# A piece of weights is begun six rooms or more behind its fetch, and its absolute value keeps its traced place in ScalarE's order

## The chip, the core and the metric

One core of a Trainium2 chip runs the whole program. The metric is the device time of one execution in microseconds; the time before is the median of three runs. TensorE (PE) multiplies, VectorE (DVE) and ScalarE (ACT) work elementwise, GpSimd (POOL) does some elementwise work and issues accumulating DMAs, SyncE (SP) issues most other DMAs.

## The reference

```python
def _attn_ref(q, k, v, lam):            # q, k, v: (2, 8, 768, 64), lam: (8,)
    for b in range(nb):                 # blocks of 64 tokens
        intra = einsum('bhic,bhjc->bhij', qb, kb) * Dmask      # Dmask: lam ** (i - j), i >= j
        intra = einsum('bhij,bhjd->bhid', intra, vb)
        inter = einsum('bhid,bhde->bhie', qb * lam_pow, kv_state)
        out[:, :, sl] = intra + inter
        kv_state = lam_block * kv_state + einsum('bhsd,bhse->bhde', kb * rev_pow, vb)
...
x = attn_out.transpose(0, 2, 1, 3).reshape(1536, 512)
h = maximum(x @ w_in, 0.0);  x = h * h @ w_out          # first MLP, 512 -> 2048 -> 512
h = x @ w_in2;  out = maximum(0.01 * h, h) @ w_out2     # second MLP
```

The four weight matrices of the two MLPs (512 x 2048 and 2048 x 512) come as float64, that is as two 32-bit words for each weight.

## The kernel before

**Stages.** First the attention part: twelve units of 128 tokens, in `retention`. Then two MLPs of four stages each, a stage being 512 of the 2048 hidden columns; tokens go in three tiles of 512. Stage (l, s) is stage s of layer l. Every product of the MLPs is three matmuls (`three`, L503): each operand is split into a high and a low part, and high*high, high*low and low*high are summed. In the second and third stage of layer 0, and in all of layer 1, pairs of tiles are multiplied with seven products in place of eight (`second_pair`, `first_pair`), which needs sums of weights (`weight_sums`, L437 to L442) and of activations (`four_sums`, L449 to L451).

**Weights.** Each of the 8 stages has four pieces of weights, 32 in all: two halves of its first matrix and two of its second. `order` lists them; they are numbered 1 to 32 here. A piece is fetched by `fetch` (1 MB, by SP's queue, into one of two buffers `raw`) and made from float64 words into a high and a low part by the generator `converting`: an absolute value on ACT (L114), six steps on DVE (L115, L116, L118, L121, L122, L125), a copy on ACT that makes the high part (L135), and a subtraction on DVE that makes the low part (L137); some pieces then, or before the copy, have their sums made. Behind L122 the raw buffer is free, and `converting` issues the next fetch, that of the piece two further on. Before the copy it waits, giving None, until `opened` holds the piece, that is until the matmuls that read the old contents of the buffer have been traced.

**Rooms.** The matmuls of the MLPs are written by generators (`first`, `first_pair`, `second_pair`, `second`) that yield after every six matmuls, half a group of twelve; each yield but those that give False is a room, in which `convert` is called once. A call gives one step of the first piece at work that has one; if none has, it begins the next fetched piece, which traces the absolute value and the first DVE step together. In the attention part there are seven rooms, at the ends of units 3 to 9 (`convert(pin=True)`), for piece 1. Rooms are numbered 1 to 355 here in the order of the calls; room 8 is the first of the MLPs.

**Order.** The program is traced in this order, and the order of each engine is then made by a planner that takes instructions when it thinks them ready, by priority, with its own idea of durations. PE's order in the MLPs is as traced (`manual_schedule`); ACT's and DVE's are the planner's. `keep_in_program_order(i)` puts instruction i behind the one that was traced just before it on the same engine. `high_priority` pulls some of the sums and splits forward. A queue runs in the order that it was given, and an instruction whose inputs aren't there holds all behind it.

Of the kernel before, what the change touches and what calls it, by code (L numbers as in the profile page):

```python
# [9 lines left out]
F32 = mybir.dt.float32  # L10
# [3 lines left out]
AF = mybir.ActivationFunctionType  # L14
# [5 lines left out]
def tile_retention_then_two_mlps(  # L20
# [12 lines left out]
    nc = tc.nc  # L33
# [30 lines left out]
    def dma(dst, src):  # L64
        return nc.sync.dma_start(dst, src)
# [7 lines left out]
    def source(l, s, n, h):  # L73
        w = ((w1, w2), (w3, w4))[l][n]
        if n == 0:
            return w[:, s * FS + h * CW:s * FS + (h + 1) * CW].rearrange("(k p) f -> p k f", p=P)
        return w[s * FS + h * CW:s * FS + (h + 1) * CW, :].rearrange("(k p) f -> p k f", p=P)
# [6 lines left out]
        order += [(*stage, 1, 0), (*stage, 0, 0), (*stage, 0, 1)]  # L84
    order.append((*stages[-1], 1, 1))
    todo = list(order)
    fetched, at_work = [], []
    wts, sums, opened = {}, {}, set()

    def fetch():  # L90
        if todo:
            key = todo.pop(0)
            r = raw.tile([P, 4 * CW], I64, tag="raw", name="raw")
            k = 4 if key[2] == 0 else 2
            dma(r.rearrange("p (k f) -> p k f", k=k), source(*key))
            fetched.append((key, r))

    def converting():
        key, r = fetched.pop(0)
        l, s, n, h = key  # L100
        k = 4 if n == 0 else 2
        words = r.bitcast(U32).rearrange("p (f t) -> p f t", t=2)
        w_lo, w_hi = words[:, :, 0], words[:, :, 1]
        ve = nc.vector
        if not apart(key):
            hb = cv.tile([P, 4 * CW], U32, tag="hb", name="hb", bufs=2)
        else:
            if h == 0:
                opened_memory[s] = late.tile([P, 2, 4 * CW], U32, tag="sw1", name="hb")
            hb = opened_memory[s][:, h]  # L110
        rb = cv.tile([P, 4 * CW], U32, tag="rb", name="rb")
        hf, rf = hb.bitcast(F32), rb.bitcast(F32)

        nc.scalar.activation(hf, w_hi.bitcast(F32), AF.Abs)  # L114
        yield ve.tensor_scalar(out=hf, in0=hf, scalar1=2.0 ** -15, scalar2=122368.0, op0=ALU.max, op1=ALU.min)  # L115
        yield ve.tensor_scalar(out=hb, in0=hb, scalar1=3, scalar2=0x3FFFFFFF,  # L116
                               op0=ALU.logical_shift_left, op1=ALU.bitwise_and)
        yield ve.scalar_tensor_tensor(out=hb, in0=w_hi, scalar=0xC0000000, in1=hb,  # L118
                                      op0=ALU.bitwise_and, op1=ALU.bitwise_or)

        yield ve.tensor_scalar(out=rb, in0=hb, scalar1=0xFF800000, scalar2=None, op0=ALU.bitwise_and)  # L121
        yield ve.scalar_tensor_tensor(out=rf, in0=w_lo, scalar=2.0 ** -52, in1=rf, op0=ALU.mult, op1=ALU.mult)  # L122
        if begun_mlp:
            fetch()
        yield ve.tensor_tensor(out=hf, in0=hf, in1=rf, op=ALU.add)  # L125
        if l == 1 and n == 0:
            w = hf.rearrange("p (k f) -> p k f", k=k)
            blocks = {(i, j): w[:, 2 * j:2 * j + 2, i * P:(i + 1) * P] for i in range(2) for j in range(2)}
            yield from weight_sums(key, f"sw{h}", blocks, rf)
        while key not in opened:  # L130
            yield None
        tags = (f"w1h{h}", f"w1l{h}") if n == 0 else ("w2h", "w2l")
        bufs = 1 if n == 0 else 3
        hi, lo = (wp.tile([P, 4 * CW], F32R, tag=tag, name=tag, bufs=bufs) for tag in tags)
        nc.scalar.copy(hi, hf)  # L135
        wts[key] = [x.rearrange("p (k f) -> p k f", k=k) for x in (hi, lo)]
        yield ve.tensor_tensor(out=lo, in0=hf, in1=hi, op=ALU.subtract)  # L137
        if (l, s) in seven and n == 1:
            while ("sums", l, s) not in opened:
                yield None  # L140
            rb = cv.tile([P, 4 * CW], U32, tag="rb", name="rb")
            w = hf.rearrange("p (k m i f) -> p k m i f", k=2, m=2, i=2)
            blocks = {(i, j): w[:, j, :, i] for i in range(2) for j in range(2)}
            yield from weight_sums(key, f"t{h + 2}", blocks, rb.bitcast(F32))
# [4 lines left out]
    def apart(key):  # L149
        return key[0] == 0 and key[1] > 1 and key[2] == 1  # L150


    def convert(pin=False):
        for piece in list(at_work):
            step = next(piece[1], False)
            if step is False:
                at_work.remove(piece)
            elif step is not None:
                if pin:
                    tc.keep_in_program_order(step)  # L160
                return
        if not fetched:
            return
        key = fetched[0][0]
        alike = sum(apart(k) == apart(key) for k, _ in at_work)
        if alike < (2 if not apart(key) or key[3] == 1 else 1):
            at_work.append((key, converting()))
            step = next(at_work[-1][1])
            if pin:
                tc.keep_in_program_order(step)  # L170
# [3 lines left out]
    begun_mlp = []  # L174
# [9 lines left out]
    def retention(ctx_att, att):  # L184
# [206 lines left out]
        for i in range(n_units):  # L391
            if i and i + 2 < n_units:
                scale_q(i + 2, transposes(i + 2))
            if i + 4 < n_units:
                load(i + 4, "kq")
            if i + 2 < n_units:
                load(i + 2, "v")
            if i in (1, 9):
                fetch()
            if i:  # L400
                if i > 1:
                    state(i)
                output(i)
                if i + 1 < n_units:
                    mask(i + 1)
                if i + 2 < n_units:
                    scores(i + 2)
            if 3 <= i <= 9:
                convert(pin=True)
# [22 lines left out]
    def weight_sums(key, tag, a, f):  # L432
        both = late.tile([P, 2, 4, 2, P], F32R, tag=tag, name="sw")
        sums[key] = both
        f = f.rearrange("p (n k f) -> p n k f", n=4, k=2)
        ve = nc.vector
        ve.tensor_tensor(out=f[:, 0], in0=a[1, 0], in1=a[1, 1], op=ALU.add)  # L437
        yield ve.tensor_tensor(out=f[:, 2], in0=a[0, 0], in1=a[1, 0], op=ALU.subtract)
        ve.tensor_tensor(out=f[:, 1], in0=f[:, 0], in1=a[0, 0], op=ALU.subtract)
        yield ve.tensor_tensor(out=f[:, 3], in0=a[0, 1], in1=f[:, 1], op=ALU.subtract)  # L440
        nc.scalar.copy(both[:, 0], f)
        yield ve.tensor_tensor(out=both[:, 1], in0=f, in1=both[:, 0], op=ALU.subtract)  # L442
# [305 lines left out]

    begun_mlp.append(True)
    fetch()  # L750
    opened.update(order[:7])
    opened.add(("sums", 0, 1))
    with tc.manual_schedule(engines={mybir.EngineType.PE}):
        for l, s in stages:
            for part in stage(l, s):
                for room in part:
                    if room is not False:
                        convert()
# [25 lines left out]
```

## Time and profile before

| | us |
|---|---|
| median of 3 runs (lowest, highest) | 576.34 (575.51, 576.9) |
| the profiled execution's own time | 577.1 |
| its span, first to last instruction | 575.3 |
| PE busy | 566.2 (98%) |
| DVE busy | 413.8 (72%) |
| ACT busy | 303.7 (53%) |
| POOL busy | 103.3 (18%) |
| mean granted TensorE clock | 0.994 |

The span is 1.8 us shorter than the execution's time. Busy times are sums over the whole span; the stages differ in which engine has room left. The profile tells for each idle time what ended it, and the timeline view has every instruction with its start.

### The profile page before, as it was taken

Reading aid. Unit: us, or ns where it says so; the run is one execution under the profiler, and the core shown is the slowest. Engines: PE = TensorE matmul, PEld = TensorE weight load, DVE = VectorE, ACT = ScalarE, POOL = GpSimd, SP = SyncE. Lnnn points to the kernel's source line nnn. Section 1 sums busy time; section 2 is a strip of 40 time slices with the busy share of each in tenths; the row PEclk is TensorE's granted clock in tenths of the full one; section 3 lists DMA queues with packets and bytes.
Section 4 is the critical chain, followed back from the end, with each engine's and each line's share of the span. In section 5 each row is a group of like instructions: output and inputs, shape, how many; then the busy total and the mean of one; then the engine's idle time right before and its main releaser. Section 6 shows DMA issues by size and latency. Waiting matters only on the chain.

```text
span 575.3 us, 8060 instructions
## 1 busy us (share of the span) xinstructions
PE 566.2 (98%) x3075; PEld 472.8 (82%) x3075; DVE 413.8 (72%) x579; ACT 303.7 (53%) x477; POOL 103.3 (18%) x115
## 2 busy tenths in 40 slices
PE   7999999999999999999999999999999999999997
PEld 6888888888788888888888888888888888888886
DVE  3588999999927599498478999929782996217222
ACT  2344598556757587757448375453562376225110
POOL 3659100000044503433000000000213010210000
PEclk9899999999999999999999999999999999999999
DMA  8998434665498957999513215341529423651432
GB/s 173 235 218 177 142 130 140 221 190 186 171 157 137 161 168 176 214 254 188 174 38 91 81 34 216 129 164 73 110 49 246 108 32 43 78 87 56 164 111 91
DMA packets 79350, 80.75 MB, mean 140 GB/s; under 512 B 40264, under 2 KB 51792, under 8 KB 79312
## 3 DMA queue, kind: packets, MB, share of 16 engines
q1 hardware_dynamic: 61312, 62.15, 35.2%
q0 software_dynamic: 17472, 17.83, 22.9%
q8 instruction: 24, 0.39, 0.3%
q10 hardware_dynamic: 528, 0.26, 0.2%
q14 instruction: 14, 0.11, 0.1%
HBM read 55.05 MB, written 30.42 MB: 149 GB/s over the span
## 4 chain that ended last, share of the span: by engine, by line
PE 79%; DVE 10%; DMA 5%; issue 3%; ACT 2%; POOL 1%; SPq 0%; ACTq 0%; POOLq 0%; DVEq 0%
PE ps L503 72%; DMA raw<-in_moe_w_in 4%; PE ps L294 2%; DMA raw<-in_moe_w_out 2%; DVE hb L118 2%; PE ps L311 1%; DVE rb L122 1%; DVE hb L125 1%; PE ps L362 1%; DVE hb L115 1%; DVE rb L121 1%; PE ps L335 1%; ACT hb L114 1%; PE ps L220 1%; PE ps L360 1%
## 5 line engine op out<-in xcount | busy, mean ns | idle before, releaser
L503 PE MATMUL ps<-xhi,w1h 128*128 128x512 f32 x288 | 112.2, 389 | 0.0
L503 PE MATMUL ps<-xhi,w1l 128*128 128x512 f32 x288 | 112.0, 389 | 0.0
L503 PE MATMUL ps<-xlo,w1h 128*128 128x512 f32 x288 | 112.0, 389 | 0.0
L616 POOL DMA_DIRECT2D spill<-f x48 | 47.1, 1194 | 348.3 <-ACT f L612 348.2
L612 ACT COPY f<-ps 128x512 f32<-128x512 f32 x84 | 48.4, 585 | 69.6 <-PE ps L503 68.8
L503 PEld LDWEIGHTS ps<-xhi,w1l 128*128 128x128 f32 x288 | 54.1, 188 | 11.3
L503 PEld LDWEIGHTS ps<-xlo,w1h 128*128 128x128 f32 x288 | 54.1, 188 | 11.3
L503 PEld LDWEIGHTS ps<-xhi,w1h 128*128 128x128 f32 x288 | 54.0, 188 | 11.3 <-issue 0.2
L474 DVE TENSOR_TENSOR g0l<-f,g0h 128x512 fp32r<-128x512 f32 x52 | 35.1, 687 | 32.5 <-ACT f L470 20.9
L503 PE MATMUL ps<-w2l,g0h 128*128 128x512 f32 (+1 forms) x132 | 50.5, 383 | 0.0
L503 PE MATMUL ps<-w2h,g0l 128*128 128x512 f32 (+1 forms) x132 | 50.5, 383 | 0.0
L503 PE MATMUL ps<-w2h,g0h 128*128 128x512 f32 (+1 forms) x132 | 50.5, 383 | 0.0
L114 ACT ACTIVATE hb<-raw 128x1024 f32<-128x1024 f32 x32 | 36.8, 1149 | 21.5 <-DVE w2l L137 8.3
L137 DVE TENSOR_TENSOR w2l<-hb,w2h 128x1024 fp32r<-128x1024 f32 x16 | 19.5, 1222 | 39.8 <-ACT w2h L135 39.8
L503 PE MATMUL ps<-g0h,w2h 128*128 128x512 f32 x104 | 40.5, 389 | 0.0
L503 PE MATMUL ps<-g0l,w2h 128*128 128x512 f32 x104 | 40.5, 389 | 0.0
L503 PE MATMUL ps<-g0h,w2l 128*128 128x512 f32 x104 | 40.5, 389 | 0.0
L122 DVE SCALAR_TENSOR_TENSOR rb<-raw,rb 128x1024 f32<-128x1024 uint32 x32 | 39.4, 1231 | 0.4
L125 DVE TENSOR_TENSOR hb<-hb,rb 128x1024 f32<-128x1024 f32 x32 | 39.4, 1231 | 0.4
L118 DVE SCALAR_TENSOR_TENSOR hb<-raw,hb 128x1024 uint32<-128x1024 uint32 x32 | 39.1, 1221 | 0.3
L567 DVE TENSOR_TENSOR f<-ps,f 128x512 f32<-128x512 f32 x40 | 26.2, 684 | 9.9 <-PE ps L503 9.9
L716 DVE TENSOR_TENSOR f<-ps,f 128x512 f32<-128x512 f32 (+1 forms) x25 | 16.7, 668 | 22.9 <-PE ps L503 22.8
(143 smaller groups left out, 1155.0 us busy)
## 6 DMA issues: line engine op xcount, KB each, us to landing
raw<-in_moe_w_in SPq DMA_DIRECT2D x16, 1024.0 KB, 5.7
raw<-in_moe_w_out SPq DMA_DIRECT2D x16, 1024.0 KB, 5.1
spill<-f POOLq DMA_DIRECT2D x48, 256.0 KB, 5.5
spill<-f SPq DMA_DIRECT2D x24, 256.0 KB, 2.8
f<-spill SPq DMA_DIRECT2D x24, 256.0 KB, 3.0
k<-in_k SPq DMA_DIRECT2D x12, 256.0 KB, 5.0
q<-in_q SPq DMA_DIRECT2D x12, 256.0 KB, 5.1
v<-in_v SPq DMA_DIRECT2D x12, 256.0 KB, 5.3
```

Of the source, the lines that this page charges most:

```text
L114: nc.scalar.activation(hf, w_hi.bitcast(F32), AF.Abs)
L118: yield ve.scalar_tensor_tensor(out=hb, in0=w_hi, scalar=0xC0000000, in1=hb, op0=ALU.bitwise_and, op1=ALU.bitwise_or)
L122: yield ve.scalar_tensor_tensor(out=rf, in0=w_lo, scalar=2.0 ** -52, in1=rf, op0=ALU.mult, op1=ALU.mult)
L125: yield ve.tensor_tensor(out=hf, in0=hf, in1=rf, op=ALU.add)
L137: yield ve.tensor_tensor(out=lo, in0=hf, in1=hi, op=ALU.subtract)
L294: nc.tensor.transpose(ps[:, p, :], src[:, 2 * p:2 * p + 2, :].rearrange("s h d -> s (h d)"), ident)
L474: nc.vector.tensor_tensor(out=glo, in0=r, in1=ghi, op=ALU.subtract)
L503: nc.tensor.matmul(ps, a, b, start=start and n == 0, stop=stop and n == len(ops) - 1, skip_group_check=again)
L567: ve.tensor_tensor(out=out, in0=ps[h, where], in1=other, op=ALU.add)
L612: nc.scalar.copy(f, src)
L616: nc.gpsimd.dma_start(dst, f, accum_op=ALU.add)
L716: nc.vector.tensor_tensor(out=a, in0=ps, in1=a, op=ALU.add)
```

## The change

Two things. A fetch notes the room from which its piece may be begun: six rooms behind the room of the fetch for those issued once the MLPs have begun, at once for the earlier ones; `convert` counts its calls and begins no piece before that. And the absolute value of every piece is put behind the ACT instruction that was traced just before it.

```diff
-    fetched, at_work = [], []
+    fetched, at_work, rooms = [], [], []
+    LAND = 6
...
             dma(r.rearrange("p (k f) -> p k f", k=k), source(*key))
-            fetched.append((key, r))
+            fetched.append((key, r, len(rooms) + LAND if begun_mlp else 0))
 
     def converting():
-        key, r = fetched.pop(0)
+        key, r, _ = fetched.pop(0)
...
-        nc.scalar.activation(hf, w_hi.bitcast(F32), AF.Abs)
+        tc.keep_in_program_order(nc.scalar.activation(hf, w_hi.bitcast(F32), AF.Abs))
...
     def convert(pin=False):
+        rooms.append(len(rooms))
         for piece in list(at_work):
...
-        if not fetched:
+        if not fetched or len(rooms) < fetched[0][2]:
             return
```

## Rows read from the trace of the kernel before

**Rows 1.** The page's first part: busy time, share, instructions.
```profile
PE 566.2 (98%) x3075; PEld 472.8 (82%) x3075; DVE 413.8 (72%) x579; ACT 303.7 (53%) x477; POOL 103.3 (18%) x115
```

**Rows 2.** Waits of PE: waiter, releaser, us in total, times, longest.
```profile
PE ps L503 <- DVE g1l L69: 0.9, 1, 0.9
PE ps L311 <- ACT qT L298: 0.4, 2, 0.2
```

**Rows 3.** Timeline of PE, start of the MLPs and stage (0, 1): start, us.
```profile
65.07 0.40 PE L503 MATMUL ps<-xhi,w1h 128*128 128x512 f32 x1
...
153.49 0.39 PE L503 MATMUL ps<-g1h,sw 128*128 128x512 f32 x1
...
153.95 0.88 PE L503 MATMUL ps<-g1h,sw 128*128 128x512 f32 x2
155.74 0.50 PE L503 MATMUL ps<-g1l,sw 128*128 128x512 f32 x1 [0.92 <-DVE g1l L69]
...
156.54 0.40 PE L503 MATMUL ps<-g1l,sw 128*128 128x512 f32 x1
```

**Rows 4.** Timeline of ACT, piece 9's absolute value and before the stop.
```profile
115.58 1.17 ACT L114 ACTIVATE hb<-raw 128x1024 f32<-128x1024 f32 x1 [1.54 <-DMA raw<-in_moe_w_out]
...
148.37 0.62 ACT L68 CAST t<-f 128x512 fp32r<-128x512 f32 x1 [1.26 <-DVE f L450]
...
150.10 0.58 ACT L482 ACTIVATE f<-ps 128x512 f32<-128x512 f32 x1
150.71 0.63 ACT L486 ACTIVATE f<-f 128x512 f32<-128x512 f32 x1
...
153.65 0.62 ACT L68 CAST g1h<-f 128x512 fp32r<-128x512 f32 x1 [1.82 <-DVE f L491]
```

**Rows 5.** Timeline of DVE before the stop.
```profile
151.80 1.22 DVE L125 TENSOR_TENSOR hb<-hb,rb 128x1024 f32<-128x1024 f32 x1
152.93 0.69 DVE L491 TENSOR_TENSOR f<-f 128x512 f32<-128x512 f32 x1
...
154.66 0.42 DVE L440 TENSOR_TENSOR rb<-hb,rb 128x256 f32<-128x256 f32 x1
155.00 0.69 DVE L69 TENSOR_TENSOR g1l<-f,g1h 128x512 fp32r<-128x512 f32 x1
```

**Rows 6.** Busy time by stretch: stretch, length, PE, PEld, DVE, ACT, POOL, clock.
```profile
60.00:155.74 95.74, 94.82 (x466) 78.41 (x460) 92.55 (x119) 65.55 (x98) 0.40 (x1) 1.00 0.48 161
155.74:180.00 24.26, 24.26 (x107) 20.08 (x108) 10.44 (x15) 16.48 (x29) 11.82 (x12) 1.00 0.92 156
```

**Rows 7.** Line 122 alone, from the start to 155.74 us.
```profile
L122 DVE SCALAR_TENSOR_TENSOR rb<-raw,rb x12: 1214/1218/1560, 47.3 to 150.1; 128x1024 f32<-128x1024 uint32 x12
```

**Rows 8.** Groups of DVE, 60 to 155.74 us: busy us, mean ns, idle before.
```profile
L115 DVE TENSOR_SCALAR hb<-hb 128x1024 f32<-128x1024 f32 x11 | 7.6, 687 | 1.4 <-ACT hb L114 1.4
L137 DVE TENSOR_TENSOR w2l<-hb,w2h 128x1024 fp32r<-128x1024 f32 x5 | 6.0, 1218 | 0.0
```

**Rows 9.** Timeline of ACT at the start of the MLPs, and piece 4's copy.
```profile
61.41 1.17 ACT L114 ACTIVATE hb<-raw 128x1024 f32<-128x1024 f32 x1 [2.47 <-DMA raw<-in_moe_w_in]
...
66.65 0.60 ACT L468 ACTIVATE f<-ps 128x512 f32<-128x512 f32 x1 [1.04 <-PE ps L503]
...
68.00 0.63 ACT L470 ACTIVATE f<-f 128x512 f32<-128x512 f32 x1
...
86.43 1.06 ACT L135 CAST w2h<-hb 128x1024 fp32r<-128x1024 f32 x1 [0.72 <-DVE hb L125]
```

**Rows 10.** Waits of ACT for fetched pieces, whole span.
```profile
ACT hb L114 <- DMA raw<-in_moe_w_in: 6.9, 4, 2.5
...
ACT hb L114 <- DMA raw<-in_moe_w_out: 4.5, 4, 1.5
```

**Rows 11.** Timelines of DVE and PE in stage (0, 2).
```profile
217.48 0.69 DVE L69 TENSOR_TENSOR g1l<-f,g1h 128x512 fp32r<-128x512 f32 x1
...
218.45 0.39 PE L503 MATMUL ps<-g1l,sw 128*128 128x512 f32 x1
```

## The prediction

> **What bounds the kernel.** I read the page's busy times first: PE is busy 98% of the span [rows 1]. The waits of PE come next. In the MLPs there is one, of L503 on a low part made by DVE; in the attention part a wait for ACT's copies shows 0.4 us in two places [rows 2]. PE's timeline gives the pace. Room 8 begins at 65.07 and room 73 at 153.49, 65 rooms in 88.42 us, so a room is 1.360 us and a matmul 0.2267; room r begins at 65.07 + 1.360 (r - 8) [rows 3]. The stop stands two lines on. From 153.95 to 156.54 there are five steps, which should take 1.13 us and take 2.59: 1.46 us are lost [rows 3]. PE's order and number of matmuls are not touched by the change. So what can be won is that 1.46 and the little in the attention part, and what can be lost is any new wait of PE.
>
> What made the stop is read from ACT and DVE together. The matmul waited for the low part by L69, which began at 155.00 behind the small weight sums (L437 to L440) [rows 5]. Its high part was copied on ACT at 153.65, after 1.82 us of waiting for L491 [rows 4]. L491 had its input at 151.34, when L486 ended [rows 4], and began at 152.93, behind the conversion step L125 [rows 5]. L482, the head of this chain, belongs to the group that ends when room 69 begins, 148.03; with ACT free it starts 0.22 us behind a group's end (66.65 against room 9 at 66.43 [rows 9]), so it could have started at 148.25. It started at 150.10, since ACT stood before that at a copy which waited for DVE [rows 4]. All of it is one thing: DVE is busy 92.55 of 95.74 us from 60 us on, then 10.44 of 24.26 [rows 6].
>
> And DVE is busy with work that nobody needs yet. By the code, PE is at room 74 when the stop ends, and calls up to room 74 have asked for L122 of pieces 1 to 10; the trace has 12 of them by then [rows 7]. Counted in the code, DVE has done ahead of its room: all six steps of pieces 11 and 12, L125 of piece 10, and sums that the code asks for in rooms 94 and 95. A piece's six steps are three of 1.22 [rows 7] and three of 0.69 [rows 8], 5.7 us; four sums of 0.42 [rows 5] are 1.7; together 11.4 + 1.2 + 1.7 = 14.3 us. The planner could do this because a piece's absolute value hung on nothing but its fetch: piece 9's, asked for in room 63 (139.87), ran at 115.58, and ACT even waited 1.54 us for its data [rows 4].
>
> **The change, part by part.** *The six rooms.* Counting calls: a fetch goes out in the room of a piece's sixth step and is for the piece two further on. If the present piece has its last step free, the next is begun two rooms on and takes seven, so the fetched one is begun nine rooms behind its fetch; if the present piece must wait, the next is begun one room on, and the fetched one seven rooms behind. I find no piece of the 30 concerned nearer than seven. The rule never says no; it costs and gives 0, on both ends, and moves no DMA in the code.
>
> *The pin.* No instruction is added; all 32 absolute values get a place behind the ACT instruction traced before them, which in the MLPs is an activation, copy or keep of the group that PE has just ended, or the copy of the piece before. So from a few us after its room, not before, can a piece be begun. Its first DVE step and the rest follow, and so does the fetch behind L122, later by as much, in SP's queue among the spills. A fetch still has the rooms above, 9.5 us or more at PE's pace, to land. Spills that stand behind a later fetch in SP's queue have nine buffers f, filled one a group (2.72 us), so some 20 us of cover: 0.
>
> *Term 1, the stop at 154.* With pieces 10 to 12 held to rooms 70, 76 and 82 (149.4, 157.6, 165.7), DVE has only piece 9 to mix into the chain. Without others the chain runs 148.25 + 0.58 (L482) + 0.63 (L486) + 0.69 (L491) + 0.62 (copy) + 0.69 (L69), 151.5 with small gaps [rows 4, 5]; it is needed at 153.49 + 4 x 0.2267 = 154.40. Cover 2.9 us, against one 1.22 step in progress ahead of each of the two DVE steps and one absolute value of 1.17 ahead on ACT, 3.6 at the worst, about half as a rule. Bounds: -1.46 and 0; I take -1.2, near the full gain, for the worst mix seldom falls together.
>
> *Term 2, the attention part.* Piece 1's absolute value stood ahead of copies that PE waited for [rows 2]; pinned, it comes behind them. Bounds -0.4 and 0; I take -0.2, since by the timeline one of the two waits stands there.
>
> *Term 3, deadlines in stage (0, 0).* Piece 2: its absolute value moves behind the last copy of the attention part, which ends about 64.3; 64.3 to 65.5 instead of 61.41 [rows 9]. Six steps 5.7, two activations' subtractions of 0.69 between them, copy 1.05, L137 1.22 [rows 8, 9]: ready at 74.9, needed in room 19, 80.0. Piece 3: pinned to the group that ends at room 15 (74.6), whose three activations end 2.2 us later (66.43 to 68.63 [rows 9]); absolute value to 78.0, ready at about 87.3, needed in room 31, 96.4. Piece 4: pinned to piece 3's copy, which ends at 86.1; absolute value to 87.2, six steps and three subtractions to 95.0, copy to 96.0, low part at 97.2; needed at room 32 and two matmuls, 98.16. Left: 0.9 us, and a set of activations (1.98 from L468's start to L470's end [rows 9]) ahead of a copy would overdraw it. Bounds 0 and +3.1 (two sets); I take 0, as in the rows of before the conversion's copy goes ahead of the next group's activations (86.43, piece 4 [rows 9]).
>
> *Term 4, stage (0, 2).* The same chain exists there: L69 ends at 218.17 and PE wants it at 218.45 [rows 11], 0.28 us. The first three steps of pieces 13 and 14 (2.6 us each), which ran before PE was at their rooms, now fall into it. One more 1.22 step ahead costs 0.94, two 2.2. Bounds 0 and +2.2; I take 0, because there too a 1.22 step already stands in the row of the chain.
>
> *Term 5, ACT's waits for fetches,* 11.4 us in eight [rows 10], mostly vanish; PE didn't wait behind them, so 0. From 155.74 on DVE has 13.8 us free in 24 [rows 6], which takes the moved steps in. From piece 6 on, the code leaves nine rooms or more, 12 us, between a piece's copy and its first use; 0.
>
> Sum: -1.2 - 0.2 = -1.4. On the profiled execution's own 577.1 that is 575.7; its time is 0.76 above the median of the three, 576.34, and against that median the forecast is 574.9.
>
> **Rivals.** *The wait only moves* (0.37): PE stops at 218 (term 4, +0.94), or the chain at 154 stays late with piece 9 in it. For it: the cover is 0.28 there, and both chains must pass a DVE that serves conversions in the planner's order. Against: nothing like it in 511 other us. Time 576.34 - 1.4 + 0.94 = 575.9, up to 576.5.
>
> *Piece 4 is late* (0.14), the slower one: two sets of activations ahead of its copies give 3.96 less 0.9 of cover, and a DVE that loses 1 us more by waiting for the copies makes 4.1; 576.34 - 1.4 + 4.1 = 579.0. It decides from 0.9 us of delay on, and outweighs the gain from 2.3.
>
> *VectorE's time is what counts* (0.06). In 60 to 155.74 it is busy 97% [rows 6]. It now idles from 62.6 to 65.5 and, in the same way before piece 3, about 2.4 us more: 5.3. If all its work up to 155 were needed there, PE would lose that: 576.34 - 0.2 + 5.3 = 581.4. The 14.3 us ahead speak against it. The Trainium skill (Perfetto Trace Analysis, Identifying the Most-Contended Engine) calls occupancy of VectorE a fair measure of how near it is to its limit, and by that rule this rival would be the forecast; the count of L122 shows an engine that is full without being needed in full.
>
> *The change does nothing:* true of the six rooms, not of the pin, by piece 9's row.
>
> **How the numbers follow.** About 0.2%, 1.15 us, can be told from no change here. Forecast 0.43, faster: 574.5 to 575.2. Wait moved 0.37, same: 575.2 to 577.5. The two slower ones 0.20. Nothing won can exceed 1.9 (576.34 - 1.9 = 574.4), and with the spread of the runs 574.0 is the low end; the high end, 579.0, reaches the late piece and leaves out VectorE's rival and the worst of that.
>
> **What would show it.** Piece 9's absolute value behind 144 us in place of 115.58; nine or ten L122 by 155.7; DVE busy about 78 in 60 to 155.74 and over 20 in the stretch behind; no wait of L503 on L69 near 154; ACT's waits for raw near none. Wrong would be a wait of L503 on L137 or L135 near 98, one on L69 near 218, or twelve L122 still.

## The result, and the profile after

The kernel after took 581.69 us (median of six, 580.69 to 583.49), the kernel before beside it 576.67 (six, 575.51 to 577.2): the ratio is 1.0095, 95% interval 1.0073 to 1.0116. The forecast was 574.9 with a range up to 579.0, so the change is 5.0 us slower where it was forecast 1.4 faster. The profiled execution of after took 580.69 us, its span 578.9.

Line numbers in the rows are those of the kernel that was run: what is L114, L122 and L503 in the kernel before is L115, L123 and L505 in the kernel after, and some experiments shift them again by one to three.

The page's busy times hardly differ from [rows 1]; the waits do. First the busy line of after, then the waits of TensorE in the MLPs and of ScalarE for fetched pieces (waiter, releaser, us in total, times, longest), to be read beside [rows 2] and [rows 10]:

```profile
PE 566.5 (98%) x3075; PEld 471.6 (81%) x3075; DVE 417.2 (72%) x579; ACT 303.7 (52%) x477; POOL 107.2 (19%) x115
```

```profile
PE ps L505 <- DVE g0l L476: 3.6, 2, 2.4
...
PE ps L505 <- ACT g0h L471: 0.4, 1, 0.4
...
ACT hb L115 <- DMA raw<-in_moe_w_out: 6.4, 2, 4.0
```

The wait for a low part by L69 is gone; waits for g0l and g0h have come. ScalarE waits for fetched pieces twice in place of eight times, 6.4 us in place of 11.4, but one of the two is the longest of either kernel. The stretches (length, PE, PEld, DVE, ACT, POOL, granted clock, DMA share, GB/s) answer to [rows 6], and line 123, the fifth of a piece's six steps, behind which its raw buffer is free, to [rows 7]:

```profile
60.00:153.90 93.90, 93.90 (x440) 77.87 (x438) 77.71 (x95) 64.04 (x95) 0.00 (x0) 1.00 0.35 119
153.90:180.00 26.10, 26.10 (x117) 21.62 (x116) 20.98 (x27) 17.42 (x30) 12.93 (x12) 1.00 1.02 230
180.00:186.00 6.00, 3.09 (x12) 1.73 (x11) 5.97 (x10) 3.38 (x6) 1.43 (x2) 1.00 1.18 165
186.00:189.30 3.30, 3.30 (x10) 2.58 (x9) 2.15 (x4) 1.53 (x2) 0.00 (x0) 0.53 1.02 334
```

```profile
L123 DVE SCALAR_TENSOR_TENSOR rb<-raw,rb x9: 1219/1226/1562, 45.6 to 149.3; 128x1024 f32<-128x1024 uint32 x9
```

Up to 154 all is as forecast: TensorE is never idle, VectorE has done nine fifth steps in place of twelve and is busy 77.71 of 93.90 us. Then TensorE is idle for 2.91 of 6 us, and behind that its clock is granted at 0.53. Its timeline (start, us):

```profile
180.37 0.39 PE L505 MATMUL ps<-g0h,w2h 128*128 128x512 f32 x1
180.89 0.50 PE L505 MATMUL ps<-g0l,w2h 128*128 128x512 f32 x1
181.22 0.40 PE L505 MATMUL ps<-g0h,w2l 128*128 128x512 f32 x1
181.98 0.50 PE L505 MATMUL ps<-g0h,w2h 128*128 128x512 f32 x1 [0.36 <-ACT g0h L471]
184.90 0.50 PE L505 MATMUL ps<-g0l,w2h 128*128 128x512 f32 x1 [2.41 <-DVE g0l L476]
185.23 0.39 PE L505 MATMUL ps<-g0h,w2l 128*128 128x512 f32 x1
...
186.48 0.63 PE L505 MATMUL ps<-g0l,w2h 128*128 128x512 f32 x1
186.91 0.63 PE L505 MATMUL ps<-g0h,w2l 128*128 128x512 f32 x1
...
189.77 0.40 PE L505 MATMUL ps<-g0h,w2h 128*128 128x512 f32 x1
```

From 180.37 to 189.77 there are 18 steps, which at 0.2267 take 4.08 us and here take 9.40: 5.3 us lost. Of these 3.7 lie ahead of 185.23, in the stops; the rest comes from matmuls 0.43 apart in the stretch granted 0.53, between stretches granted 1.00. In the same way a stop near 249 costs 1.75. Lost 7.1, won 1.46 [rows 3]: 5.6 us more, against 5.0 in the medians. The two profiles bear the sum out: from the first matmul of the MLPs to the last it is 507.6 us before (63.59 to 571.18) and 513.2 after (61.87 to 575.10). Their spans differ by 3.6 only, since the attention part of this execution of after was 1.7 us shorter and its end 0.4.

What made the stop stands ten microseconds ahead of it. ScalarE, then VectorE:

```profile
168.33 0.60 ACT L470 ACTIVATE f<-ps 128x512 f32<-128x512 f32 x1 [2.13 <-PE ps L505]
168.96 0.64 ACT L471 ACTIVATE g0h<-f 128x512 fp32r<-128x512 f32 x1
173.60 1.12 ACT L115 ACTIVATE hb<-raw 128x1024 f32<-128x1024 f32 x1 [4.01 <-DMA raw<-in_moe_w_out]
174.62 0.63 ACT L472 ACTIVATE f<-f 128x512 f32<-128x512 f32 x1
...
182.30 0.63 ACT L472 ACTIVATE f<-f 128x512 f32<-128x512 f32 x1
```

```profile
163.02 1.22 DVE L123 SCALAR_TENSOR_TENSOR rb<-raw,rb 128x1024 f32<-128x1024 uint32 x1
...
174.76 0.69 DVE L116 TENSOR_SCALAR hb<-hb 128x1024 f32<-128x1024 f32 x1 [5.00 <-ACT hb L115]
175.37 0.68 DVE L476 TENSOR_TENSOR g0l<-f,g0h 128x512 fp32r<-128x512 f32 x1
...
183.03 1.21 DVE L126 TENSOR_TENSOR hb<-hb,rb 128x1024 f32<-128x1024 f32 x1
184.16 0.68 DVE L476 TENSOR_TENSOR g0l<-f,g0h 128x512 fp32r<-128x512 f32 x1
```

At 173.60 stands the absolute value (L115) of piece 12. It waited 4.01 us for its fetch, between the second and the third activation of a group (L471, L472). VectorE was held as well, 5.00 us, by the first step of the same piece (L116), with the group's low part (L476) behind it. Both engines then worked off a queue for ten microseconds, VectorE 5.97 of 6 us, and the low part that TensorE wanted at 182.2 began at 184.16, behind L126; the activation that it reads (L472) had ended on ScalarE only at 182.93. The issue of the fetch (SyncE's queue: start, us; the second of the two is the next piece's, some 4 us on) and its landing (KB, median us to landing):

```profile
164.27 4.64 SPq L65 DMA_DIRECT2D raw<-in_moe_w_out  x2
```

```profile
raw<-in_moe_w_out SPq DMA_DIRECT2D x1, 1024.0 KB, 9.3
```

It went out when VectorE had done L123 of piece 10 (163.02 + 1.22), which the code asks for in room 74, with the fetch behind it in room 75, and took 9.3 us to land. In the kernel before this fetch was issued at 132.09:

```profile
132.09 0.38 SPq L65 DMA_DIRECT2D raw<-in_moe_w_out  x1
```

Piece 17 has the same ahead of the stop near 249: its absolute value, at 243.97, waits 2.36 us.

### The profile page after: what moved, and what is told of

Its sections match the earlier page's. It is cut to its first block, busy times and chain, and to the rows that moved or that the text cites. A ratio compares the mean times of both kernels' runs of the same rounds, so it can differ in the third digit from the quotient of the medians.

```text
span 578.9 us, 8048 instructions
## 1 busy us (share of the span) xinstructions
PE 566.5 (98%) x3075; PEld 471.6 (81%) x3075; DVE 417.2 (72%) x579; ACT 303.7 (52%) x477; POOL 107.2 (19%) x115
## 4 chain that ended last, share of the span: by engine, by line
PE 83%; DVE 8%; DMA 4%; issue 2%; ACT 2%; POOL 1%; ACTq 0%; POOLq 0%; DVEq 0%
PE ps L505 75%; DMA raw<-in_moe_w_out 3%; PE ps L313 2%; PE ps L296 2%; PE ps L364 2%; PE ps L362 1%; DMA v<-in_v 1%; DVE hb L119 1%; DVE rb L123 1%; PE ps L337 1%; DVE rb L122 1%; PE ps L222 1%; DVE w1l L138 1%; ACT hb L115 1%; DVE hb L116 1%
## 5 line engine op out<-in xcount | busy, mean ns | idle before, releaser
L618 POOL DMA_DIRECT2D spill<-f x48 | 52.7, 1267 | 343.7 <-ACT f L614 343.7
L505 PE MATMUL ps<-xhi,w1h 128*128 128x512 f32 x288 | 112.2, 389 | 0.0
L505 PE MATMUL ps<-xlo,w1h 128*128 128x512 f32 x288 | 112.1, 389 | 0.0
L505 PE MATMUL ps<-xhi,w1l 128*128 128x512 f32 x288 | 112.0, 389 | 0.0
L505 PEld LDWEIGHTS ps<-xhi,w1h 128*128 128x128 f32 x288 | 54.1, 188 | 11.4 <-issue 0.2
L505 PEld LDWEIGHTS ps<-xhi,w1l 128*128 128x128 f32 x288 | 54.1, 188 | 11.3
L505 PEld LDWEIGHTS ps<-xlo,w1h 128*128 128x128 f32 x288 | 54.1, 188 | 11.2
L505 PE MATMUL ps<-w2l,g0h 128*128 128x512 f32 (+1 forms) x132 | 50.5, 383 | 0.0
L505 PE MATMUL ps<-w2h,g0l 128*128 128x512 f32 (+1 forms) x132 | 50.5, 383 | 0.0
L505 PE MATMUL ps<-w2h,g0h 128*128 128x512 f32 (+1 forms) x132 | 50.5, 383 | 0.0
L505 PE MATMUL ps<-g0l,w2h 128*128 128x512 f32 x104 | 41.6, 400 | 3.8 <-DVE g0l L476 3.6
L476 DVE TENSOR_TENSOR g0l<-f,g0h 128x512 fp32r<-128x512 f32 x52 | 35.0, 686 | 11.0 <-ACT f L475 9.2
L505 PE MATMUL ps<-g0h,w2h 128*128 128x512 f32 x104 | 41.3, 397 | 0.4 <-ACT g0h L471 0.4
L505 PE MATMUL ps<-g0h,w2l 128*128 128x512 f32 x104 | 41.0, 395 | 0.0
L115 ACT ACTIVATE hb<-raw 128x1024 f32<-128x1024 f32 x32 | 36.4, 1139 | 7.0 <-DMA raw<-in_moe_w_out 6.4
L126 DVE TENSOR_TENSOR hb<-hb,rb 128x1024 f32<-128x1024 f32 x32 | 39.5, 1234 | 0.7
L123 DVE SCALAR_TENSOR_TENSOR rb<-raw,rb 128x1024 f32<-128x1024 uint32 x32 | 39.5, 1233 | 0.6
L116 DVE TENSOR_SCALAR hb<-hb 128x1024 f32<-128x1024 f32 x32 | 22.1, 691 | 15.9 <-ACT hb L115 15.8
```

What stands on the lines that cost most here:

```text
L115: tc.keep_in_program_order(nc.scalar.activation(hf, w_hi.bitcast(F32), AF.Abs))
L476: nc.vector.tensor_tensor(out=glo, in0=r, in1=ghi, op=ALU.subtract)
L505: nc.tensor.matmul(ps, a, b, start=start and n == 0, stop=stop and n == len(ops) - 1, skip_group_check=again)
L618: nc.gpsimd.dma_start(dst, f, accum_op=ALU.add)
```

## The experiments

All are the kernel after but for the edit shown; the kernel before ran beside each, and ratios are to it. Two theories stood first. A: the absolute values of pieces 12 and 17 are pinned ahead of their data. B: VectorE, its work now bunched behind 154, is overloaded there. From the second group on, theory C: the fetch is late because the earlier pieces are pinned, and the absolute value stands ahead of its data whoever puts it there.

**The rooms alone.** The pin is taken off:

```diff
-        tc.keep_in_program_order(nc.scalar.activation(hf, w_hi.bitcast(F32), AF.Abs))
+        nc.scalar.activation(hf, w_hi.bitcast(F32), AF.Abs)
```

> The rule of six rooms alone, no absolute value pinned. The count of rooms says that the rule never holds a piece back: every theory in which the pin is the cause expects the time of before, 576.7 (576.0 to 577.4), with the stop of PE near 154 us back. If the rule costs anything, 578 or more.

576.39 us, ratio 0.9992 (0.9974 to 1.001). The order on every engine is that of the kernel before. The six rooms do nothing; all that happened is the pin's. The stop near 154 is back, but costs 0.55 us in this trace where it cost 1.45 in that of the kernel before: with one and the same order it differs that much from execution to execution.

**The pin on all but two, on those two alone, and sixteen rooms for them.** In the first two `tc.keep_in_program_order` is called only where the condition holds; the third changes the distance.

```diff
+        if order.index(key) + 1 not in (12, 17):        # the first
+        if order.index(key) + 1 in (12, 17):            # the second
-            fetched.append((key, r, len(rooms) + LAND if begun_mlp else 0))
+            fetched.append((key, r, len(rooms) + (16 if order.index(key) + 1 in (12, 17) else LAND) if begun_mlp else 0))   # the third
```

> All absolute values pinned but those of pieces 12 and 17, the two that waited for their data (4.01 and 2.36 us). Theory A (a pinned absolute value whose fetch is late stands at the head of ScalarE and holds the activations behind it): the stops of PE near 180 and 249 us go with their 3.7 + 1.8 (half clock) + 1.6 us = 7.1, the stop near 154 stays away; 581.7 - 7.1 = 574.6 (574.0 to 575.4), which is faster than before. Theory B (VectorE has too much moved work from 155 us on, and the low parts are late by that): stops of PE on g0l remain, 579 or more.

582.61 us, ratio 1.0085 (1.0054 to 1.0116): a miss. ScalarE's timeline shows why. Without a pin the planner puts piece 12's absolute value at the very same place, and by the traces every engine and every DMA queue has the order of the kernel after. The wait is there again:

```profile
170.56 0.63 ACT L473 ACTIVATE g0h<-f 128x512 fp32r<-128x512 f32 x1
175.74 1.13 ACT L115 ACTIVATE hb<-raw 128x1024 f32<-128x1024 f32 x1 [4.54 <-DMA raw<-in_moe_w_out]
176.76 0.62 ACT L474 ACTIVATE f<-f 128x512 f32<-128x512 f32 x1
```

> Only the absolute values of pieces 12 and 17 pinned. Theory A: their fetches are late only because the pins before them made VectorE reach L123 of piece 10 and of piece 15 late; with the others free the fetches go out as before (near 132 and 217 us), nothing waits at the head of ScalarE, and the time is that of before, 576.7, or down to 575.3 if the stop near 154 goes with piece 12. If the pin on these two is the cost by itself: 580 or more, with a stop near 180.

584.17 us, ratio 1.0112 (1.0082 to 1.0141): a second miss for A. The time is that of the other case, the pin on these two as the cost by itself, but not its mechanism. Piece 12 doesn't wait here; two unpinned pieces fetched behind it do. The first of the two, piece 14, is fetched at 172.35, when L125 (the fifth step, here) of the pinned piece 12 has ended at 172.28; in the kernel before it was fetched at 151.35. ScalarE:

```profile
180.36 1.12 ACT L115 ACTIVATE hb<-raw 128x1024 f32<-128x1024 f32 x1 [2.94 <-DMA raw<-in_moe_w_in]
...
213.57 1.11 ACT L115 ACTIVATE hb<-raw 128x1024 f32<-128x1024 f32 x1 [3.50 <-DMA raw<-in_moe_w_in]
```

> All pinned, but pieces 12 and 17 may be begun 16 rooms behind their fetch in place of 6, that is from rooms 91 and 139 in place of 82 and 134. Theory A: their data has landed by then, ScalarE waits less than 1 us for it, both stops go; 574.6 (574.0 to 575.6). Theory B: the same work on VectorE falls later still, into rooms 91 to 101; 579 or more.

574.99 us, ratio 0.9957 (0.9941 to 0.9973): faster than both kernels. TensorE has no wait in the MLPs, ScalarE none for a fetch. VectorE has the same work, piece 12's steps some 6 us later, and nothing is late, which speaks against B. A's remedy is right and its cause wrong: the pins of pieces 12 and 17 are not what holds them ahead of their data. That made theory C.

**Which pins make the fetch late.** The pin on pieces 9 to 11 alone, and on all others:

```diff
+        if 9 <= order.index(key) + 1 <= 11:             # the one
+        if not 9 <= order.index(key) + 1 <= 11:         # the other
```

> Only the absolute values of pieces 9, 10 and 11 are pinned; all others are left to the planner. Theory C (the cost of the change comes from the fetch of piece 12, which goes out behind the sixth VectorE step of piece 10 and so later when piece 10 is pinned, and from its absolute value then standing at the head of ScalarE before the data is there, whoever put it there): the stop near 154 is gone (-1.45), piece 12's absolute value waits about 4 us for its data, TensorE stops near 182 with half clock behind it (+5.5): 576.7 - 1.45 + 5.5 = 580.7, up to 582.3 if piece 17 waits too. Rival (a piece waits because of its own pin): no wait of piece 12, 576.7 - 1.45 = 575.2.

585.65 us, ratio 1.0146 (1.0118 to 1.0174): as C has it in kind, but a miss in size, 3 us above the range. Piece 12, unpinned, waits 7.3 us for a fetch issued at 165.13, and later pieces wait too:

```profile
ACT hb L115 <- DMA raw<-in_moe_w_in: 12.4, 5, 5.9
ACT hb L115 <- DMA raw<-in_moe_w_out: 9.6, 3, 7.3
```

By TensorE's timeline 6.4 us are lost from 180 to 192 and 3.5 from 218 to 229; with the 1.45 won, 577.23 + 8.4 makes 585.6.

> All absolute values are pinned but those of pieces 9, 10 and 11. Theory C: pieces 9 to 11 run early again, so piece 12's fetch goes out early, near 136 us as in the kernel before, its absolute value doesn't wait and the stop near 182 with its half clock (5.5 us) is gone; the stop near 154 is back (+1.45); piece 17 still waits for its data near 244 (1.6 us stay): 581.7 - 5.5 + 1.45 = 577.65, between 576.2 and 579. Rival (a piece waits because of its own pin): piece 12 waits as in the kernel after, 581.7 + 1.45 = 583.1.

578.5 us, ratio 1.0026 (1.0002 to 1.0051), within what was expected. Piece 12's fetch goes out at 154.97, not near 136 as I had written, which is still early enough: its absolute value doesn't wait. The stop near 154 didn't come back; another of 1.5 us stands near 164, mostly on a high part by ScalarE (L68). 0.35 is lost at 183, and piece 17's wait, 2.94 here, costs 3.9 with a stretch at half rate.

**The fetch one step later.** For pieces 12 and 17 the call of `fetch` is moved behind the last VectorE step:

```diff
-        if begun_mlp:
+        late_fetch = order.index(key) + 1 in (10, 15)
+        if begun_mlp and not late_fetch:
             fetch()
         yield ve.tensor_tensor(out=hf, in0=hf, in1=rf, op=ALU.add)
+        if late_fetch:
+            fetch()
```

> The kernel after, with the two fetches in dispute, those of pieces 12 and 17, issued one VectorE step later (behind the last step of pieces 10 and 15 in place of the one before it); everything else stands. Theory C (TensorE pays for the time by which the data of these two pieces is late): each lands 1.2 us or more later, the waits of ScalarE for raw grow from 6.4 us by 2.4 or more, and TensorE's stops near 182 and 249 grow by about as much: 581.7 + 2.4 = 584.1, between 583 and 587. Rival (the stop near 182 comes from VectorE's load or from the order of the engines, and the data's delay is hidden): no change, 581.7.

581.9 us, ratio 1.0068 (1.0045 to 1.0091). The edit didn't do what it was for: the transfer still goes out when L123, the last reader of its buffer, is done (VectorE and SyncE):

```profile
164.54 1.21 DVE L123 SCALAR_TENSOR_TENSOR rb<-raw,rb 128x1024 f32<-128x1024 uint32 x1
```

```profile
165.78 4.64 SPq L65 DMA_DIRECT2D raw<-in_moe_w_out  x2
```

Every engine and queue has the order of the kernel after. So it tells nothing for or against the rival; my expectation had forgotten that the buffer, not the place in the code, sets the issue.

**The transfers beside the fetch.** Eighteen of GpSimd's accumulating transfers of stage (0, 1) are left out, so that the output lacks what they add:

```diff
             accums.append(dst)
-            nc.gpsimd.dma_start(dst, f, accum_op=ALU.add)
+            if len(accums) > 8:
+                nc.gpsimd.dma_start(dst, f, accum_op=ALU.add)
...
-                nc.gpsimd.dma_start(dst, src, accum_op=ALU.add, max_dma_last_dim=TT)
+                if s != 1:
+                    nc.gpsimd.dma_start(dst, src, accum_op=ALU.add, max_dma_last_dim=TT)
```

> The kernel after, with GpSimd's eighteen accumulating transfers of stage (0, 1) left out, so that its output lacks what they add; the order of the other engines is that of the kernel after. The fetch of piece 12 then has the DMA engines nearly to itself. Theory C with a long landing (the fetch takes 9.3 us because it shares the DMA engines with these transfers; fetches elsewhere take 4.7 to 5.6): issued near 164.3, it lands near 169.6, piece 12's absolute value waits 0.5 us at most, and the stop near 182 with its half clock (5.5) is gone: 581.7 - 5.5 = 576.2, between 575 and 577.5. Rival (the fetch goes out too late, and its landing doesn't matter): wait and stop stay, 581.7.

576.02 us, ratio 0.9993 (0.998 to 1.0005), as expected. The order of every engine but GpSimd is that of the kernel after, so VectorE has the same queue; the stop near 183 is gone, and with that B falls. The fetch lands in 4.9 us (KB, median us to landing), and piece 12's absolute value, at the same place in ScalarE's order, has no wait:

```profile
raw<-in_moe_w_out SPq DMA_DIRECT2D x1, 1024.0 KB, 4.9
```

```profile
171.42 1.11 ACT L115 ACTIVATE hb<-raw 128x1024 f32<-128x1024 f32 x1
```

Nearly half of the 9.3 us is the company: in the nine us from its issue the DMA engines' share is 1.06 in the kernel after (164.3 to 173.3) and 0.78 here (166.2 to 175.2). The 4.7 to 5.6 us of the expectation fit the fetches between 60 and 152 us; others in the kernel after take up to 10.2 (issued at 239.68). The Trainium skill (DMA: Bandwidth & Descriptors, Issuing engines are not separate DMA queues) says that transfers started by different engines run on the same 16 DMA engines and interleave; the two landings agree.

**How far behind the fetch.** Twelve rooms for every piece from 9 on:

```diff
+            fetched.append((key, r, len(rooms) + (LAND if order.index(key) < 8 else 12) if begun_mlp else 0))
```

> The kernel after, with every piece from 9 on begun twelve rooms or more behind its fetch in place of six, all pinned. Piece 12 is then begun in room 88 instead of 82, about 8 us later, piece 17 in room 139 instead of 134. Theory C: by the profile of the kernel after, piece 12's data is there at 173.3 us, and room 88 begins near 170.7 with some 2 us of activations ahead: a wait of at most 1 us, no stop near 182, none near 249: 575.0, between 574.0 and 576.2, as with sixteen rooms for pieces 12 and 17 alone. Rival (the distance only helps those two, and beginning the others later delays them past their use): 577 or more, with waits of TensorE on weights.

574.98 us, ratio 0.9968 (0.9952 to 0.9984): faster than before, and equal to sixteen rooms for two pieces. These are all the waits of TensorE that its view lists; none is in the MLPs:

```profile
PE ps L337 <- POOL qS L306: 2.1, 1, 2.1
PE ps L222 <- POOL pw L227: 1.5, 1, 1.5
PE ps L362 <- DVE st L349: 0.6, 2, 0.3
PE ps L313 <- ACT qT L300: 0.2, 1, 0.2
```

Then piece 12 alone at nine, ten and twelve rooms:

```diff
+            land = 9 if order.index(key) == 11 else LAND     # then 10, then 12
+            fetched.append((key, r, len(rooms) + land if begun_mlp else 0))
```

> The kernel after, with piece 12 alone begun nine rooms behind its fetch (room 84) in place of seven (room 82). Theory C, as a dose: in the profile of the kernel after, piece 12's absolute value waits 4.01 us and TensorE loses 5.5 us near 182 to 189 (3.7 in stops, 1.8 at half clock), piece 17's waits 2.36 and TensorE loses 1.6. A begin two rooms, 2.7 us, later leaves a wait of about 1.3 us for piece 12, and by the same relation a stop of about 0.6 without half clock; piece 17's stays: 581.7 - 5.5 + 0.6 = 576.8, between 575.8 and 578. Rival (the stop doesn't follow the wait, or it needs ten rooms more as with sixteen): 580 or more.

582.75 us, ratio 1.0117 (1.0101 to 1.0132): a miss, since the absolute value stands between the same two activations as with seven rooms. The pin only says what the absolute value comes behind; up to nine rooms it stands where the planner puts it with no pin at all, as the run with all but 12 and 17 pinned showed. Here too the order on every engine is that of the kernel after.

> Nine rooms left piece 12's absolute value at the very place of the kernel after in ScalarE's order, between the second and the third activation of one group, so that dose never took. With ten rooms (room 85) it stands one instruction later, behind that third activation and ahead of a copy and the next group's three. Theory C (what counts is the time by which ScalarE is held, with all that stands behind it): the third activation is done in the time that was waited, so the wait shrinks by its 0.6 us, and TensorE loses some 0.6 less than after: 581.1, between 579.5 and 582. Rival (only the one activation that stood right behind the absolute value was late): the stop near 182 with its half clock, 5.5 us, is gone: 576.2.

582.23 us, ratio 1.0097 (1.0068 to 1.0125), just above what was expected: one more activation ahead of the wait saved nothing that can be told.

> With twelve rooms for piece 12 alone (room 88), its absolute value stands behind that group's third activation, a copy and the next group's first activation. By the profile of the kernel after these end near 172.2 us and the data is there at 173.3. Theory C: a wait near 1.1 us, from which TensorE loses about 0.4 (piece 17's waits of 2.4 to 3.3 cost it 0.7 less than their length), no half clock; piece 17's 1.6 stay: 581.7 - 5.5 + 0.4 = 576.6, between 575.8 and 577.8. Rival (all three activations of the next group have to be ahead too): 579 or more.

576.96 us, ratio 1.0005 (0.9988 to 1.0021), as expected. The second and the third, on ScalarE (different kernels):

```profile
171.07 0.63 ACT L473 ACTIVATE f<-f 128x512 f32<-128x512 f32 x1
175.43 1.13 ACT L116 ACTIVATE hb<-raw 128x1024 f32<-128x1024 f32 x1 [3.73 <-DMA raw<-in_moe_w_out]
```

```profile
172.26 0.59 ACT L471 ACTIVATE f<-ps 128x512 f32<-128x512 f32 x1
174.28 1.12 ACT L116 ACTIVATE hb<-raw 128x1024 f32<-128x1024 f32 x1 [1.43 <-DMA raw<-in_moe_w_out]
```

**Wait and loss side by side.** Waits are ScalarE's for the piece; what TensorE lost is worked out from its timeline around the stop, as above (first start to last, less 0.2267 for each matmul). The runs with pins on 12 and 17 alone and on 9 to 11 alone, where other pieces wait too, are left out. All in us.

| kernel | piece 12 waits | lost near 183 | piece 17 waits | lost near 249 |
|---|---|---|---|---|
| no accumulating transfers | 0 | 0 | 1.17 | 0.57 |
| twelve rooms, piece 12 | 1.43 | 1.23 | 2.29 | 1.69 |
| after | 4.01 | 5.34 | 2.36 | 1.75 |
| pins on all but 12 and 17 | 4.54 | 5.76 | 2.44 | 1.87 |
| nine rooms, piece 12 | 3.11 | 5.93 | 2.87 | 2.24 |
| ten rooms, piece 12 | 3.73 | 6.32 | 3.11 | 2.73 |
| fetch a step later | 3.65 | 4.97 | 3.32 | 2.69 |
| pins on all but 9 to 11 | 0 | 0.35 | 2.94 | 3.9 |

Four of these rows are one order of instructions: after, the pins on all but 12 and 17, nine rooms, and the fetch a step later. They are not doses, but the same order timed four times (581.69, 582.61, 582.75 and 581.9 us), and their waits of 3.1 to 4.5 us and losses of 5.0 to 5.9 show how much one order varies from execution to execution. For piece 12 the other rows go from no wait and a loss of 0 or 0.35 through 1.43 and 1.23 to 3.73 and 6.32 with ten rooms. Each loss of 5 us or more has a stretch at half rate in it, and its length differs with the order the same (9 matmuls in after, 14 with nine rooms). What sets that length is open.

For piece 17 the loss is the wait less 0.4 to 0.6 in the first seven kernels. In the last it is 0.9 more than the wait; there a stretch at half rate (granted 0.50 from 249.2 to 252.3) stands behind the stop.

## Why the prediction was wrong

**The step that failed** is in the sentences on the pin and Term 5: "A fetch still has the rooms above, 9.5 us or more at PE's pace, to land", and "ACT's waits for fetches, 11.4 us in eight, mostly vanish; PE didn't wait behind them, so 0". The rooms lie between two places in the code; the transfer and the absolute value don't both keep to them. The sentence before had it right that the fetch goes out later with L123, by as much as the piece is held. Room 8 began at 63.38 us in the profile of after, so room 70 at 147.7, room 75 at 154.5 and piece 12's room 82 at 164.0 (1.360 us a room). Piece 10, begun in room 70, is pinned behind the copy of piece 9 (152.32 on ScalarE), and its absolute value began at 153.28, 5.6 us behind its room; its L123 ended at 164.24, 9.7 us behind the room of the fetch. So the 9.5 us were used up when the transfer was issued, and 9.3 us of landing stood against what ScalarE had ahead of the absolute value. The term was 0; it measured 5.3 near 183 and 1.75 near 249. Piece 17 shows that it isn't the number of rooms alone: its fetch belongs to room 123 and its beginning to room 134, eleven rooms or 15 us, but the transfer went out at 236.44, 11.3 us behind the start of room 123 (225.16), and took 7.4 us.

I had also taken the rows of before for more than they say: eight waits for fetches, none above 2.5 us, cost TensorE nothing there; I take it, though no run shows it by itself, that the pieces ran so early that nothing wanted stood behind them. With pieces held to their rooms, a group's activations stand there, on ScalarE and by L116 on VectorE.

**Term 1** held: no wait of L505 on L69 near 154, nine fifth steps, 77.71 us busy up to there against 78 forecast, 20.98 behind. Piece 9's absolute value ran at 143.65 where I had said behind 144; the MLPs began 1.7 us earlier in this profile. With the fetch cured, two other kernels come to 574.98 and 574.99 us, against the 574.9 of the forecast. That the levels agree so closely is in part luck: by the ratios they gain 1.8 and 2.5 us on the kernel before beside them, not 1.4. In their traces the MLPs take 506.1 us from first matmul to last, 1.5 less than in that of the kernel before.

**The six rooms** give 0, as worked out; as a distance they are too short to bind, and with twelve, from piece 9 on, they cure what the pin does.

**Term 3** held: piece 4's low part was ready at 94.56 (93.33 + 1.23) and first wanted at 96.50 (room 32 and two matmuls, as in the prediction), 1.94 us left where I had 0.9. **Term 4** held: TensorE has no wait near 218. **Term 2** can't be told from one trace each: the MLPs begin at 63.1 to 63.8 us in the four kernels without a pin on piece 1 and at 61.9 to 65.2 in the ten with it. TensorE's largest waits in the attention part, which [rows 2] leaves out, are for GpSimd: 2.4 and 1.5 us before, 2.3 and 1.5 after.

**Rivals.** The slower cases that I priced, piece 4 and VectorE's time, are not what happened; that VectorE's 97% was no need is now shown, since it is busy 14.8 us less up to 154 and nothing there is late. "The wait only moves" had the right idea at the wrong place and price.

## What to carry to other kernels

A distance between a fetch and its use that is counted in the program's order is worth only what is left of it when the transfer is issued: look up what frees the buffer, when that instruction ends, and how long the landing takes among the other transfers of that stage, and compare with the end of the work ahead of the use in its queue. Before pinning an instruction that waits for a transfer, name what stands behind it on its engine and behind its first consumer on the next. When work is held back to keep an engine free, its fetch is held back too, and the distance has to grow with it: here the rule of six rooms had to become one of twelve.

## What the runs showed of the hardware

A stop can cost more than itself. In the kernel after 3.7 us of stops were followed by four steps at the full pace (185.23 to 186.13) and then by nine longer ones, seven of them 0.43 us, in a stretch granted 0.53, before 1.00 came back: 1.6 us more, at or near the lower of the two levels, 1.2 GHz. The single stop of 1.5 us near 249 had none behind it; in the kernel with pins on all but 9 to 11, stops of 0.5 and 1.5 us, close together from 245.5 to 248.6, had. The Trainium skill (TensorE: Matmul & The Clock Gate, Wait — 56ns, not 53.3ns?) gives, from start to start for 512 columns, 426.7 ns at 1.2 GHz and 215.7 ns at 2.4 GHz. The 0.43 us here agrees with the first; at granted clock 1.00 this kernel holds 0.2267 us, which is longer than the second, and the sums here go by what was measured.

The same 1 MB fetch took 4.9 us to land without GpSimd's accumulating transfers beside it; with them it took 9.3 us in the kernel after and 8.4 to 9.8 in the three others of the same order. With them left out the kernel took 576.02 us in place of 581.69.
